# A fused mLSTM cell and squared-ReLU FFN on one NeuronCore: five groups of steps move to other places in the program

## The chip, the cores and the metric

The kernel runs on 1 core of one Trainium2 chip. The metric is the device time of one execution in microseconds (us). Before the change the median of 6 runs is 491.36 us, from 490.32 to 494.64.

A NeuronCore has five instruction streams. PE (TensorE) multiplies matrices into PSUM banks. DVE (VectorE), ACT (ScalarE) and POOL (GpSimd) do elementwise work. SP (SyncE) here only issues DMAs. Each stream runs in the order in which it was written, so an instruction that waits holds up all that stand behind it on its engine, and the engines wait for one another through semaphores.

## The reference

All inputs are float32. The attention part is a recurrence over 768 time steps for 4 batches x 8 heads, with head size 40:

```python
for t in range(S):
    m_new = np.maximum(f[t] + m, i[t])
    f_stab, i_stab = np.exp(f[t] + m - m_new), np.exp(i[t] - m_new)
    C = f_stab * C + i_stab * outer(v[t], k[t])      # 40 x 40 state of each head
    n = f_stab * n + i_stab * k[t]
    y[t] = sigmoid(o[t]) * (C @ q[t]) / np.maximum(np.abs(n @ q[t]), 1.0)
```

Its output is reordered to 3072 tokens x 320 features (8 heads x 40) and goes through an FFN: `h = max(x @ w_in, 0)`, `out = (h * h) @ w_out`, with w_in 320 x 2048 and w_out 2048 x 320. The launcher hands the weights over as 64-bit words: their raw bits are fetched as two 32-bit words each and put together on the chip.

## The kernel before, in words

**Tiling.** Time is cut into 24 chunks `s` = 0..23 of 128 tokens (6 per batch, batch by batch). Within a chunk the recurrence is written in its parallel form: scores k.q, weighted by decays, times the values, plus the state C carried from the chunk before times the queries. The FFN works on 12 groups `g` of two chunks.

**What is done for a chunk.** `load_part` and `load` fetch k, q, v; `transposes` turns k and q on PE, with the copies to SBUF on ACT; `load_A` brings the cumulated decays, broadcast to all partitions; `mask` (POOL) makes them causal; `weigh` takes their exponentials (ACT) and makes `vw`, the weighted values (POOL); `scores` is PE; `weighted` multiplies scores and weights (DVE); `attend` does the products with the values and with the state, on PE; `decay_old` is POOL; `half_tanh` is the output gate's sigmoid (ACT) on what `load_o` fetched; `normalise` makes the chunk's output x (DVE); `turn_rows` turns x on PE and copies it to `xT` on ACT. From chunk 4 on, other forms of the same steps are used (`attend_begin`, `attend_end`, `normalise_turned`), with turns by way of DRAM.

**Weights.** The class `Rounding` goes through 18 pieces: pieces 0 to 9 are w_in (0, 1, 3, 4, 5, 6, 8, 9 are 128 rows x 512 columns; 2 and 7 are `w_in2`, the last 64 rows, fetched by two DMAs), pieces 10 to 17 are w_out. Each piece has three steps that may stand far apart: `fetch` (SP: the DMA of the raw words), `words` (ACT: two instructions, lines 216 and 218) and `join` (DVE: three instructions, lines 227, 231, 232; then one POOL add, line 236, which writes the weight; and then the fetch of a later piece, since a raw buffer is free). Of the raw buffers three are in turn, and pieces 3, 7 and 11 use a fourth place inside `lent_t`.

**FFN.** `ffn1(g, pp)` is a quarter of x @ w_in for group g: 16 matmul passes at line 896 and 8 at line 907, into two PSUM banks of `ps_h` (3 banks). `relu_half` empties these banks on ACT and `square_half` squares. For groups 0 and 1 this is plain; from group 2 on FFN1 is `ffn1_open`, `ffn1_rows` and `ffn1_close`, and from group 1 on FFN2 is `ffn2_fast`. These need fewer products, at the price of sums of weights (`sums_of_weights(0..3)`, `sums_of_win`) and of activations (`sums`) on DVE. `sums_of_weights(3)` writes one quarter of w_out in place (line 961).

**Order.** Everything is in an order written out by hand, and each engine and SP's queue run in that order. There are three stretches:

1. The opening (lines 1148 to 1223): chunks 0 and 1 whole, chunk 2 begun, pieces 0 to 3 of the weights. `idle(n)` are n matmuls on zeros.
2. The loop over `u` = 0..7 (from line 1228): in each, a quarter of FFN1 of group 0 or 1, half of a chunk's attention (chunks 2 to 5), and pieces of the weights up to the count in `NEXT`. `rounding.step()` does words one piece ahead and a join.
3. The main loop over `n` (from line 1345): part n is (which, g, i), with `which` 1 for FFN1 and 2 for FFN2 of group g; the chunk is s = 6 + n // 4, and `at` = n % 4 says which of its steps go with the part.

The steps that the change touches: the fetch of piece 2 and `load_part(2, ...)` in SP's order; `load_A(3)` and `load_part(3, ...)`; `scores(0)`; `scores(2)`; `weigh(1)`; words and joins 1 to 3; `load_o(4)` to `load_o(7)` in the loop over u; `half_tanh(6)` and `half_tanh(7)`; the two POOL clears of the state buffers `C_flat` (line 1200); `sums_of_weights(3)` (line 961); and `spread_slots(2)` (three DMAs on POOL's queue).

Of the kernel before, what the change touches and what calls it, by code (L numbers as in the profile page):

```python
# [29 lines left out]
def kernel(  # L30
# [148 lines left out]
    class Rounding:  # L179
# [11 lines left out]
        def fetch(self):  # L191
            n = len(self.raws)
            if n == len(pieces):
                return
            dst, srcs = pieces[n]
            if n < LENT and n % NRAW == NRAW - 1:
                at = 2 * NPAIR * P
                raw = lent_t[:, at : at + 2 * WIDE].bitcast(I32).rearrange("p (c w) -> p c w", w=2)
            else:
                raw = conv.tile([P, WIDE, 2], I32, name="raw", bufs=NRAW - 1)  # L200
            self.raws.append(raw)
            for rows, src in srcs:
                to = raw[rows, : dst.shape[1]]
                if len(src.shape) == 4:
                    to = to.rearrange("p (a f) w -> p a f w", a=src.shape[1])
                nc.sync.dma_start(to, src)
# [200 lines left out]
    def load_o(s):  # L407
        b, c = divmod(s, NB)
        r, (s0, s1) = next((r, (a, z)) for r, (a, z) in enumerate(RUNS) if a <= s < z)
        if s == s0:  # L410
            st["og", r] = ld.tile([P, 4, H, D], F32, name="og")
        og = st.setdefault(s, {})["og"] = st["og", r][:, s - s0]
        nc.sync.dma_start(og, o_gate[b, :, c * P : (c + 1) * P, :].rearrange("h p d -> p h d"))
# [25 lines left out]
    def spread_mask(s):  # L439
        H2 = H // 2  # L440
        A = ps_h.tile([P, H2, P], F32, name="A_ps", tag="h_ps")
        nc.tensor.matmul(
            A[:], lhsT=ident_h[:], rhs=later_h[:].unsqueeze(1).to_broadcast([P, H2, P]), start=True, stop=True,
            skip_group_check=True,
        )
        st.setdefault(s, {}).setdefault("A", []).append(A)
# [688 lines left out]
    def idle(n):  # L1135
        t = ps_h.tile([P, W], F32, name="idle", tag="h_ps")
        for _ in range(n):
            nc.tensor.matmul(
                t[:], lhsT=zeros[:, :1].to_broadcast([P, P]), rhs=zeros[:, :1].to_broadcast([P, W]), start=True, stop=True,
            )  # L1140
# [5 lines left out]
    def load_part(s, i):  # L1146
        b, c = divmod(s, NB)
        dst, src = load_parts(s)[i]
        nc.sync.dma_start(dst, src[b, :, c * P : (c + 1) * P, :].rearrange("h p d -> p h d"))
# [10 lines left out]
    load_part(1, 2)  # L1160
    load_o(0)
    load_o(1)
    idle(12)
    transposes(0)
    idle(4)
# [3 lines left out]
    rounding.words()  # L1169
    store_A()  # L1170
    load_A(2)
    load_part(2, 0)
    load_part(2, 1)
    fetch(1)
    load_part(2, 2)
    fetch(1)
    spread_A(0)
    turn_gates(i_sb, b_T)
    rounding.join()
    load_A(3)  # L1180
    load_part(3, 0)
    load_part(3, 1)
    eA_turned = turn_gates(A_sb, eA_T, later=True)
    weigh(0)
    eA_turned()
    transposes(1, (False, True))
    spread_mask(1)
    spread_mask(1)
    spread_A(1)
    scores(0)  # L1190
    weigh(1)
    scores(1, (True, True))
    rounding.words()
    first.close()
    ffn = ctx.enter_context(tc.tile_pool(name="ffn", bufs=2))
    before = ExitStack()
# [2 lines left out]
    for x in C_flat:  # L1199
        nc.gpsimd.memset(x[:], 0.0)  # L1200
    C_old += [x[:, : 2 * PR * D1].rearrange("p (j i d) -> p j i d", i=2, d=D1) for x in C_flat]
    half_tanh(0)
    half_tanh(1)
    weighted(0)
    weighted(1)
    attend(0)
    rounding.join()
    load_part(3, 2)
    load_o(2)
    load_o(3)  # L1210
    rounding.words()
    normalise(0)
    attend(1)
    rounding.join()
    turn_rows(0)
    transposes(2)
    idle(2)
    turn_rows(1)
    rounding.words()
    scores(2)  # L1220
    weigh(2, masked=True)
    decay_old(2)
    rounding.join()


# [2 lines left out]
    for u in range(8):  # L1228
        s = 2 + u // 2
        relu_half()  # L1230
        if u % 2 == 0:
            if u == 0:
                ffn1(0, 0)
            else:
                if u == 2:
                    idle(3)
                if s - 1 < X_SQ:
                    turn_rows(s - 1)
                if u == 4:
                    square_half()  # L1240
                scores(s)
                ffn1(u // 4, u % 4)
            if u == 2:
                rounding.words()
                weigh(4, masked=True, vw=False)
                decays(4)
                rounding.words()
            weighted(s)
            if u == 0:
                mask(s + 1)  # L1250
                rounding.step()
            if u == 2:
                rounding.join()
                rounding.join()
                mask_W(4)
                values(4)
                rounding.words()
            else:
                if u == 0:
                    relu_half()  # L1260
                weigh(s + 1, masked=(u != 6), vw=(u == 6))
                if u == 4:
                    mask_W(5)
                square_half()
                if u > 0:
                    scale_q(s)
        else:
            if u == 1:
                half_tanh(2)
                half_tanh(3)  # L1270
            if u < 7:
                load_A(s + 2)
            for r in {1: (), 3: (5, 6), 5: (7,), 7: ()}[u]:
                load(r)
            if u == 5:
                for r in range(4, 8):
                    half_tanh(r)
            if s < X_SQ:
                attend(s)
            else:  # L1280
                attend_begin(s)
                attend_end(s)
                store_num(s)
            if u == 3:
                square_half()
            if u != 3:
                rounding.join(fetch=u < 7)
            if u == 1:
                load(4)
                values(s + 1)  # L1290
            if s < X_SQ:
                normalise(s)
            if u == 3:
                rounding.join()
            if u == 5:
                pair_up(7)
            if u == 7:
                load_A(7)
            if u > 4:
                load_num(s)  # L1300
            transposes(s + 1, (True, True))
            rounding.words()
            ffn1(u // 4, u % 4)
            if u != 3:
                square_half()
            if u == 5:
                decays(5)
            if u == 7:
                normalise_turned(4)
                store_rows(4)  # L1310
                rounding.fetch()
                rounding.join()
        if u < 4:
            load_o(4 + u)
        while rounding.done < NEXT[u]:
            if u == 1 and rounding.done + 1 == NEXT[u]:
                rounding.join()
            else:
                rounding.step()
        if u == 6:  # L1320
            load_squares(7)
        for x in WIN_SUMS.get(u, ()):
            sums_of_win(x)
# [21 lines left out]
    for n, (which, g, i) in enumerate(parts):  # L1345
# [3 lines left out]
            late = ctx.enter_context(tc.tile_pool(name="late", bufs=1, side="right"))  # L1349
        even = s % 2 == 0  # L1350
        fast = which == 1
        if at == 0 and even:
            do(scores, s)
            if n > 0:
                do(turn_kq, s + 1)
            do(weighted, s)
# [5 lines left out]
            rounding.join()  # L1362
        if at == 1:
            do(attend_begin, s)
            if even:
                do(lambda s: scores(s, ("h", "h")), s + 1)
            if fast:
                ffn1_rows(g, 0, True)
            do(attend_end, s)
            do(decays, s + 1)  # L1370
            do(mask, s + 1)
            if not even and not fast:
                do(turn_kq, s + 1)
            do(decay_C, s + 1)
            if not fast and not even:
                do(turn_squares, s - 1)
            if even and s > NB:
                do(load, s + 3)
            do(store_num, s)
            if n == 1:  # L1380
                normalise_turned(5)
                store_rows(5)
                turn_squares(4)
            if n == 5:
                load_rows(6)
            do(load_num, s)
            if n == 1:
                load_rows(5)
                weigh(7, masked=True)
                sums_of_win(2)  # L1390
            do(load_squares, s + 2)
            if even:
                do(load_A, s + 2)
# [4 lines left out]
        if n == 8:  # L1398
            sums(1, slice(0, NPAIR), (3,))
        if n == 9:  # L1400
            sums_of_weights(3)
            sums(1, slice(0, NPAIR), (4,))
            sums_of_weights(2)
            turn_squares(6)
# [67 lines left out]
            sums_of_weights(1)  # L1472
        if n == 3:
            turn_halves()
        if n in (9, 25):
            spread_slots(2 + n // 25)
        if at == 0:
            ffn1_square()
# [33 lines left out]
```

## Time and profile before

| what | before |
|---|---|
| time, median of 6 runs | 491.36 us |
| time, lowest to highest | 490.32 to 494.64 us |
| the profiled execution's own time | 489.87 us |
| its span, first to last instruction | 488.2 us |
| PE busy | 478.6 us (98%) |
| PE weight loads busy | 446.7 us (92%) |
| DVE busy | 339.2 us (69%) |
| ACT busy | 242.7 us (50%) |
| POOL busy | 225.8 us (46%) |
| mean granted TensorE clock | 0.996 |

The profile is one execution. Times in it count from its first instruction. A line of the timeline names start, length, engine, source line, operation, out<-in, shape and count, and in brackets the engine's idle time just before and what ended it. "PE" are matmuls, "PEld" the weight loads beside them, "SPq" the queue of SP. The difference of 1.7 us between the execution's own time and its span lies outside the instructions. The matmuls of float32 operands appear as two passes each.

### The profile page before, as it was taken

How to read it: one execution, taken by the hardware profiler on the slowest of the kernel's cores; microseconds unless marked ns; L12 is line 12 of the kernel's file. 1: busy time of each engine (PE TensorE's matmuls, PEld its weight loads, DVE VectorE, ACT ScalarE, POOL GpSimd, SP SyncE). 2: the span in 40 equal slices, each digit the busy share in tenths (PEclk: the TensorE clock that was granted, in tenths of full speed). 3: DMA queues.
4: the chain of work that ended last, by engine and by line, in shares of the span. 5: the costliest groups of instructions: out<-in, count | busy, mean ns of one | idle time of the engine just before them, and what ended most of it. 6: DMA issues, size and time to landing. Idle time of an engine off the chain costs nothing.

```text
span 488.2 us, 15402 instructions
## 1 busy us (share of the span) xinstructions
PE 478.6 (98%) x6227; PEld 446.7 (92%) x6229; DVE 339.2 (69%) x719; ACT 242.7 (50%) x534; POOL 225.8 (46%) x335
## 2 busy tenths in 40 slices
PE   9999999999999999999999999999999999999997
PEld 4877887779989999999999999998999999999997
DVE  7778768896986856857966956866956956635441
ACT  4479899534842741942742941742942650513300
POOL 5454534664689078089089077189074040020000
PEclk9989999999999999999999999999999999999999
DMA  8999998769999668769669759779646512200000
GB/s 180 195 233 239 306 212 206 207 120 210 190 141 219 123 113 219 139 112 213 130 110 220 132 93 214 144 129 206 121 93 164 122 48 83 56 21 10 1 28 27
DMA packets 192695, 69.92 MB, mean 143 GB/s; under 512 B 158128, under 2 KB 181360, under 8 KB 192624
## 3 DMA queue, kind: packets, MB, share of 16 engines
q1 hardware_dynamic: 186400, 58.68, 56.8%
q0 software_dynamic: 6080, 10.16, 9.4%
q8 instruction: 49, 0.80, 0.7%
q14 instruction: 22, 0.18, 0.1%
q10 hardware_dynamic: 144, 0.10, 0.1%
HBM read 55.69 MB, written 18.92 MB: 153 GB/s over the span
## 4 chain that ended last, share of the span: by engine, by line
PE 87%; DVE 4%; DMA 3%; ACT 2%; SPq 2%; issue 1%; POOL 0%; DVEq 0%; ACTq 0%; POOLq 0%
PE h_ps L980 34%; PE h_ps L1056 25%; PE h_ps L1089 7%; PE h_ps L896 5%; PE h_ps L934 4%; PE numT L746 3%; PE numT L727 2%; PE numT L757 1%; PE h_ps L907 1%; PE h_ps L579 1%; DMA raw<-in_moe_w_out_dram 1%; PE tp L579 1%; DMA a_rows<-A_sb 1%; DMA raw<-in_moe_w_in_dram 1%; PE tp L587 1%
## 5 line engine op out<-in xcount | busy, mean ns | idle before, releaser
L478 POOL TENSOR_SCALAR_AFFINE_SELECT A_bc<-A_bc 64x512 f32<-64x512 f32 x32 | 23.5, 733 | 89.0 <-ACT kq L496 71.0
L1070 ACT COPY r_sb<-h_ps 128x512 f32<-128x512 f32 x20 | 11.7, 586 | 85.5 <-PE h_ps L1056 85.5
L980 PE MATMUL h_ps<-T,S 128*128 128x160 f32 x352 | 51.7, 300 | 0.0
L980 PE MATMUL h_ps<-w_out,g 128*128 128x160 f32 x336 | 49.4, 303 | 0.7 <-DVE w_out L961 0.7
L980 PEld LDWEIGHTS h_ps<-T,S 128*128 128x128 f32 x352 | 48.9, 190 | 0.4 <-ACT g_c L1105 0.2
L980 PEld LDWEIGHTS h_ps<-w_out,g 128*128 128x128 f32 x336 | 46.1, 190 | 2.3 <-DVE w_out L961 0.9
L996 DVE TENSOR_TENSOR y_sb<-y_sb,h_ps 128x160 f32<-128x160 f32 x44 | 14.0, 319 | 45.3 <-PE h_ps L980 44.9
L1056 PE MATMUL h_ps<-xT,w_in 128*128 128x128 f32 x320 | 43.3, 278 | 0.0
L1056 PE MATMUL h_ps<-lent_t,w_in 128*128 128x128 f32 x320 | 42.3, 275 | 0.0
L1056 PEld LDWEIGHTS h_ps<-xT,w_in 128*128 128x128 f32 x320 | 39.2, 192 | 1.6 <-issue 1.2
L375 POOL DMA_DIRECT2D va<-in_v_dram x64 | 39.2, 619 | 1.4 <-DMA kq_rows<-in_k_dram 0.8
L1089 PE MATMUL h_ps<-xT,w_in 64*64 64x128 f32 x960 | 39.1, 272 | 0.0
L1056 PE MATMUL h_ps<-lent_t 128*128 128x128 f32 x320 | 39.0, 275 | 0.0
L1056 PEld LDWEIGHTS h_ps<-lent_t,w_in 128*128 128x128 f32 x320 | 38.9, 192 | 0.0
L1056 PEld LDWEIGHTS h_ps<-lent_t 128*128 128x128 f32 x320 | 37.3, 192 | 0.0
L509 ACT ACTIVATE A_bc<-A_bc,b_R 128x64 f32<-128x64 f32 (+1 forms) x128 | 35.7, 361 | 1.1 <-POOL A_bc L478 0.7
L1089 PEld LDWEIGHTS h_ps<-xT,w_in 64*64 64x64 f32 x960 | 34.8, 133 | 1.3
L780 DVE STREAM_TRANSPOSE tn<-numT 128x256 f32<-128x256 f32 x36 | 14.0, 428 | 30.2 <-PE numT L727 21.1
L896 PE MATMUL h_ps<-xT,w_in 128*128 128x256 f32 x128 | 31.2, 398 | 1.1 <-ACT g L920 0.8
L1048 POOL TENSOR_TENSOR lent_t<-xT 128x128 f32<-128x128 f32 (+1 forms) x18 | 14.7, 833 | 32.7 <-DVE xT L862 32.7
L896 PEld LDWEIGHTS h_ps<-xT,w_in 128*128 128x128 f32 x128 | 24.6, 199 | 5.5 <-POOL w_in L236 1.0
L980 PE MATMUL h_ps<-w_out,g_c 128*128 128x160 f32 x192 | 28.0, 302 | 0.0
(223 smaller groups left out, 1146.4 us busy)
## 6 DMA issues: line engine op xcount, KB each, us to landing
A_bc<-a_slots SPq DMA_DIRECT2D x32, 256.0 KB, 4.5
kq<-num_rows SPq DMA_DIRECT2D x80, 64.0 KB, 2.3
num_rows<-tn SPq DMA_DIRECT2D x18, 256.0 KB, 2.6
raw<-in_moe_w_out_dram SPq DMA_DIRECT2D x7, 640.0 KB, 5.6
kqT<-kq_rows SPq DMA_DIRECT2D x34, 128.0 KB, 4.0
og<-in_o_gate_dram SPq DMA_DIRECT2D x24, 160.0 KB, 4.7
x_rows<-x_sb SPq DMA_DIRECT2D x20, 192.0 KB, 3.0
xT<-x_rows SPq DMA_DIRECT2D x80, 48.0 KB, 3.7
```

The lines of the kernel that those rows point to most:

```text
L375: eng.dma_start(dst[HALVES[n], PR * (1 - late_keys) : PR * (2 - late_keys)], src[HALVES[late_keys], PR * m : PR * (m + 1)],)
L478: nc.gpsimd.affine_select(part, part, compare_op=ALU.is_ge, fill=-1e30, base=0, pattern=[[0, PR], [0, 2], [1, DP]], channel_multiplier=-1,)
L509: nc.scalar.activation(A[0][:, x, to], A[0][:, x, to], AF.Exp, bias=b_R[:, b, c, own, x : x + 1],)
L746: nc.tensor.matmul(d["numT"][m][HALVES[e], i, t0:], lhsT=va_w[s % NKQ][keys, at * D1 : at * D1 + DP], rhs=rhs, start=(s % NB == 0 and i == ...
L780: nc.vector.transpose(to[:, 2 * m : 2 * m + 2], d["numT"][m].rearrange("p c t -> p (c t)"))
L896: nc.tensor.matmul(hs[i][:, n, :], lhsT=w_in[:, a, fb * P : (fb + 1) * P], rhs=xT[:, :, a, :], start=(n == 0 and a == 0), stop=False,)
L934: nc.tensor.matmul(st["o_ps"][j], lhsT=st["g2", 0][:, fb, j * P : (j + 1) * P], rhs=w_out[:, fb, :], start=(fb == 0), stop=(fb == NF - 1),)
L980: nc.tensor.matmul(to, lhsT=lhsT[:, p], rhs=rhs[:, p, :], start=(start and p == 0), stop=(p == NPAIR - 1), skip_group_check=True,)
L996: add = lambda to, a, b: nc.vector.tensor_tensor(to, a, b, op=ALU.add)
L1048: sub = lambda to, a, b: eng.tensor_tensor(to, a, b, op=ALU.subtract)
L1056: nc.tensor.matmul(to[:, n, :], lhsT=lhsT[:, 4 * q + n, :], rhs=rhs, start=(start and n == 0), stop=True, skip_group_check=True,)
L1089: nc.tensor.matmul(to[cols, n, :], lhsT=w_in2[rows, 4 * q + n, cols], rhs=rhs, start=(start and n == 0), stop=True, skip_group_check=True,)
```

## The change

The program's instructions are the same in kind; they stand in other places.

- **Opening.** SP issues the fetch of piece 2 and chunk 2's k and q before `load_A(2)`, not after it. `load_A(3)` and chunk 3's k and q come behind `weighted(1)`. `scores(0)` stands before the masks of chunk 1. words 1 stand before `weigh(1)` and join 1 before `attend(0)`. The clears of `C_flat` stand before `weigh(1)`. words 2 stand right behind `weighted(1)` in ACT's order; words 3 stand behind `weigh(2)`. `transposes(2)` follows `turn_rows(1)`.
- **Loop over u.** `scores(2)` follows `ffn1(0, 0)`. `load_o(4)` to `load_o(7)` stand in u = 2 and u = 3, two in each, instead of one in each of u = 0..3. `half_tanh(6)` and `half_tanh(7)` leave u = 5.
- **Main loop.** `half_tanh(6)` and `half_tanh(7)` are in part 2. `sums_of_weights(3)` is in part 5, between `attend_begin` and `attend_end` of chunk 7, instead of part 9. `spread_slots(2)` is in part 12 instead of part 9.

```diff
     load_o(0)
     load_o(1)
+    fetch(1)
+    load_part(2, 0)
+    load_part(2, 1)
     idle(12)
...
     store_A()
     load_A(2)
-    load_part(2, 0)
-    load_part(2, 1)
-    fetch(1)
     load_part(2, 2)
     fetch(1)
     spread_A(0)
     turn_gates(i_sb, b_T)
     rounding.join()
-    load_A(3)
-    load_part(3, 0)
-    load_part(3, 1)
     eA_turned = turn_gates(A_sb, eA_T, later=True)
     weigh(0)
     eA_turned()
     transposes(1, (False, True))
+    scores(0)
     spread_mask(1)
     spread_mask(1)
     spread_A(1)
-    scores(0)
-    weigh(1)
-    scores(1, (True, True))
-    rounding.words()
     first.close()
...
         nc.gpsimd.memset(x[:], 0.0)
...
+    rounding.words()
+    weigh(1)
+    scores(1, (True, True))
     half_tanh(0)
     half_tanh(1)
     weighted(0)
+    rounding.join()
+    attend(0)
     weighted(1)
-    attend(0)
+    load_A(3)
+    load_part(3, 0)
+    load_part(3, 1)
+    rounding.words()
+    normalise(0)
+    attend(1)
     rounding.join()
     load_part(3, 2)
     load_o(2)
     load_o(3)
-    rounding.words()
-    normalise(0)
-    attend(1)
-    rounding.join()
     turn_rows(0)
-    transposes(2)
     idle(2)
     turn_rows(1)
-    rounding.words()
-    scores(2)
+    transposes(2)
     weigh(2, masked=True)
     decay_old(2)
+    rounding.words()
     rounding.join()
...
             if u == 0:
                 ffn1(0, 0)
+                scores(2)
...
             if u == 5:
-                for r in range(4, 8):
-                    half_tanh(r)
+                half_tanh(4)
+                half_tanh(5)
...
-        if u < 4:
-            load_o(4 + u)
+        if u in (2, 3):
+            load_o(2 * u)
+            load_o(2 * u + 1)
...
+        if n == 2:
+            half_tanh(6)
+            half_tanh(7)
...
             do(attend_begin, s)
+            if n == 5:
+                sums_of_weights(3)
...
         if n == 9:
-            sums_of_weights(3)
             sums(1, slice(0, NPAIR), (4,))
...
-        if n in (9, 25):
+        if n in (12, 25):
             spread_slots(2 + n // 25)
```

## The prediction, made before the result was known

> **What bounds the kernel now.** I read the page first, then PE's waits, then the chain that ended last for the first 110 us, then the timelines of ACT, SP, DVE and PE around the places where the chain leaves PE, and last the windows with the granted clock.
>
> ```profile
> PE 478.6 (98%) x6227; PEld 446.7 (92%) x6229; DVE 339.2 (69%) x719; ACT 242.7 (50%) x534; POOL 225.8 (46%) x335
> ```
>
> PE is the bound: busy for 98% of a span of 488.2 us. Moving steps can only win PE's idle time, a slowed clock and the fillers. PE's waits, the longest first:
>
> ```profile
> PE tp L870 <- ACT xT L875: 1.4, 1, 1.4
> PE idle L1138 <- DVE zeros L1133: 1.0, 1, 1.0
> PE h_ps L896 <- ACT g L920: 0.8, 1, 0.8
> ```
>
> The second is the start of the run. Smaller ones are 0.7 for line 961 on DVE and 0.2 for a copy to xT at 61.98.
>
> The chain says what is behind the first: from 14.13 it runs through SP's queue, the raw words of piece 2, ACT, and only at 26.06 into PE.
>
> ```profile
> 14.13 0.34 SPq L434
> ...
> 16.27 2.84 SPq L206
> 19.15 4.22 DMA raw<-in_moe_w_in_dram
> ...
> 26.06 1.24 PE tp L587 x16
> ```
>
> ACT stands 6.00 us in front of words 2, and behind it wait the two copies to xT that PE needs. Later it stands 1.18 us in front of words 7, behind which the emptying of PSUM banks (line 920) waits, and 2.14 us for piece 10.
>
> ```profile
> 23.46 0.66 ACT L216 ACTIVATE lent_t<-raw 128x512 f32<-128x512 f32 x1 [6.00 <-DMA raw<-in_moe_w_in_dram]
> ...
> 44.10 0.68 ACT L216 ACTIVATE mag<-lent_t 128x512 f32<-128x512 f32 x1 [1.18 <-DMA lent_t<-in_moe_w_in_dram]
> 44.69 0.65 ACT L218 ACTIVATE low<-lent_t 128x512 f32<-128x512 uint32 x1
> 45.25 1.06 ACT L920 ACTIVATE g<-h_ps 128x512 f32<-128x512 f32 x2
> ```
>
> The windows give the clock. In 24.0 to 27.0 PE was busy 1.75 of 3.00 us (58%), and it then ran 3.4 us at half clock; in 44.1 to 47.5 it was busy 2.56 of 3.40 (75%), and the clock stayed.
>
> ```profile
> 24.00:27.00 3.00, 1.75 (x22) 1.34 (x22) 1.93 (x5) 2.42 (x6) 0.81 (x1) 1.00 0.96 362
> 27.00:30.40 3.40, 3.40 (x12) 2.57 (x11) 1.61 (x4) 3.37 (x10) 0.46 (x1) 0.50 0.94 188
> ...
> 44.10:47.50 3.40, 2.56 (x23) 2.24 (x24) 2.62 (x4) 3.40 (x7) 1.64 (x2) 1.00 1.17 284
> ```
>
> **The opening, part by part.** *Piece 2's fetch earlier.* SP's last issue before its wait for a_rows ends at 12.99, and it stands until 14.13. The two fetches of piece 2 (issues 2.84 and 0.61, landing 4.22 after the later one) now go there instead of 16.27. With issues of 0.6 to 1.4 they land near 18.5 to 19.5 instead of 23.38. Words 2 (1.2 us on ACT) end near 20.5. Chunk 2's k and q follow (1.09 and 0.58); `load_A(2)` moves behind four issues, from 14.13 to about 16 to 18.5, and with the 5.3 us to landing that its neighbours show, from 19.4 to 21.5 to 24. Behind it wait mask 2 on POOL (1.35 us, at 20.89 so far), then join 2's add (1.27), chunk 2's exponentials (ACT, at 28.16 so far). They are needed near 26 and 28.5, so the cover is 2 us; were the load still later, each us would fall on the first FFN1 part.
>
> *Words 1 before weigh 1; join 1, attend 0 sooner; scores 0 first.* Scores 0 (half of 2.06 us) put chunk 1's mask products 1.0 us later, so weigh 1 (2.3 us) starts at 14.3 instead of 13.31; in front of it words 1 (1.3 us) fit into just that time. On DVE, weighted 0 starts at 12.6 instead of 14.41, and join 1 (1.6 us) fits into the 2.15 us that DVE stood idle. Chunk 1's x, done at 23.8, comes near 23.0. The clears (0.72 on POOL) go into a gap of 1.55 and cost nothing. The xT copies then wait for no words: turn of chunk 1 near 23.3 instead of 25.09, `transposes(2)` (1.09) behind it, first FFN1 part at 25.1 instead of 27.23. That is 2.1 us; without a 1.4 us gap before it I expect no half clock, which spares half of 3.4, 1.7 us.
>
> Join 2's fetch (piece 6) now stands ahead of chunk 3's v and two gate loads in SP's queue and can hold them until join 2 ends, near 25.2; SP, still held by chunk 3's k and q until 26.0 in the profile (3.43 at 22.57), should come no sooner: 0, and for each us that join 2 is later, sigmoids 2 and 3 are later too.
>
> *Scores 2 behind the first FFN1 part*: 1.2 us of PE work inside the count either way. Weighted 2 (1.29 on DVE) now comes between scores 2 and the products with it, covered by the state products ahead of them on PE (1.05 + 0.89 = 1.94). Without that cover it costs up to 1.3.
>
> *Where this gain goes.* From 27.23 PE worked 17.9 us until it was ready for the third FFN1 part at 45.13; now 17.9 - 1.7 + 1.2 = 17.4, so from 25.1 it is ready at 42.5. But that part started at 45.97 for another reason: words 7 could start at 44.10, then came bank emptying and PE. Raw words 7 stand behind the same DMAs as before, in another order (piece 5 before the decays, k and q of chunk 3; piece 6 before chunk 3's v and two gate loads). They land earlier only by transfer time no longer wasted. The windows of 1 us from 14 to 21 have DMA shares of 0.82, 0.85, 0.91, 0.90, 1.24, 0.25 and 0.82: 1.45 us free. Lower bound: 0, if the free time only moves. Upper: 42.5 instead of 45.97, 3.5 us, where PE's own work binds. I take 1.7: nearest to the 1.45 measured, and a little for raw words 7 no longer standing right behind raw words 6.
>
> **Loop over u.** Moving `load_o(4)` and `load_o(5)` (0.43 and 0.59 of SP, 160 KB each) out of u = 0 and 1 brings raw words 10 forward, so ACT's 2.14 us wait shrinks by more than the 1.7 and the 0.22 us wait of PE at 61.98 goes: 0.2. In u = 2 and 3 these loads stand ahead of chunk 5's decays (line 434 at 54.81), which ACT takes at 62.73: some 0.8 us of SP and transfer, against the 1.7 won. Sigmoids 6 and 7 take 1.9 us off ACT at 70.12; no PE wait stood there: 0.
>
> **Main loop.** Part 5: line 961 took 1.96 us (its neighbours at 954 and 956 took 1.48), put where DVE stood 2.00 us idle, then another 0.90:
>
> ```profile
> 116.62 0.78 DVE L780 STREAM_TRANSPOSE tn<-numT 128x256 f32<-128x256 f32 x2 [2.00 <-PE numT L727]
> ...
> 136.70 1.96 DVE L961 TENSOR_TENSOR w_out<-w_out 128x1280 f32<-128x1280 f32 x1
> ```
>
> ```profile
> 138.71 2.44 PE L980 MATMUL h_ps<-w_out,g 128*128 128x160 f32 x16 [0.68 <-DVE w_out L961]
> ```
>
> Cost 0; without the cover, 2.0. In part 9 PE's 0.68 us goes; next in DVE's order are the sum at 138.58 and T2 at 139.99, needed by PE at 145.3 and 143.2 and now 1.9 earlier: 0.7 won. Sigmoids 6 and 7 in part 2 (1.9 us) lie in ACT's 7.58 us before 108.26: 0. `spread_slots(2)` (0.59 + 1.20 on POOL) leaves 143.39 for about 151, ahead of chunk 12's decays by tens of us; mask 10 moves from 157.07 by up to 1.8, and its exponentials are first needed past 170: 0.
>
> **Sum.** 1.7 + 0.2 + 0.7 = 2.6 us off the profiled execution's 489.87 us: 487.3. That execution is 1.5 us below the median of the runs, 491.36, so the median should come to 488.8 us, 0.53% less. About 0.5%, 2.5 us, is what a measurement of this kernel can tell from no change, so the forecast lies at that bound.
>
> **A rule against the row.** The Trainium skill, page "TensorE: Matmul & The Clock Gate", Part 1, says that the array falls to half clock after at least one idle window of about 3.4 us. By that rule the wait in front of the third FFN1 part (44.3 - 42.5 = 1.8 us) costs no clock, and the sum stays at 2.6. The row shows half clock after a window that was 58% busy; by the row such a wait can cost 1.7, and the sum would be 0.9. The row decides; hence the rivals below.
>
> **Rivals.**
> - *PE's own work binds as far as part 3* (raw words 7 in time): 3.5 + 0.2 + 0.7 = 4.4, 487.0 us. For it: 1.45 us of free transfer time, and ACT 2.68 us less in front of words 5. Against: the set of transfers ahead is the same.
> - *Hidden anyway*: raw words 7 land at 44.0 as before, the opening's gain is all waited away; 0.2 + 0.7 remain: 490.5 us. For it: DMA share near or above 1 from 21 to 28 and 40 to 47.
> - *Slower: half clock in front of the third FFN1 part.* If raw words 7 do not land before about 43.5, PE, ready at 42.5, stands 3 us or more; a window under 58% busy follows, and PE runs at half clock for one window (1.7) or, if the gap spreads over two, two (3.4). With 0.9 won, that is +0.8 to +2.5: 492.2 to 493.9 us. Against: the fillers and the turn of chunk 2 lie in the same window.
>
> **How the numbers follow.** Forecast, gain of 1.8 to 3.4 (488.0 to 489.6): 0.46, of it 0.30 below 488.9 and 0.16 above. PE-bound: 0.17, faster. Hidden: 0.23, no change. Slower: 0.14, of it 0.13 past 0.5% with the half that spreads and the misses of cover above (2.0 at part 5, 1.3 at weighted 2), 0.01 within. Sum: faster 0.47, within 0.40, slower 0.13. Range: from 486.7 (PE-bound, less 0.3 for the scatter of medians) to 492.4, with the lower end of the slower case; about 1 in 10 beyond each end.
>
> **What would show it.** Right: ACT's 6.00 us before words 2 down to some 2 and no clock of 0.50 near 27 to 30; first FFN1 matmul near 25; third near 44.3, released by ACT line 920; no PE wait on line 961, and DVE's idle before 116 filled. Wrong: a granted clock of 0.5 between 40 and 50; raw words 7 landing at 44 still; PE waiting on xT or mask 2; DVE late for the turns of chunk 7.

## The result, and the profile after

| what | before | after |
|---|---|---|
| time, median (runs) | 490.35 us (78) | 487.85 us (38) |
| time, lowest to highest | 487.44 to 494.64 us | 484.87 to 491.82 us |
| ratio, 95% interval | | 0.9952, 0.9939 to 0.9966 |
| the profiled execution's own time | 489.87 us | 486.68 us |
| its span | 488.2 us | 485.0 us |
| PE busy | 478.6 us | 475.8 us |

The change takes off 2.5 us (0.48%, between 0.34% and 0.61%); between the two profiled executions it is 3.2. The forecast was 488.8, with a range of 486.7 to 492.4. Five executions of the calls below, four of 612 to 1243 us and one of 495.75, stand outside the ratios and the clock counts.

PE's line of the page, and the head of PE's waits (line waited for, total us, times, longest):

```profile
PE 475.8 (98%) x6227; PEld 445.1 (92%) x6229; DVE 341.1 (70%) x719; ACT 243.3 (50%) x534; POOL 229.3 (47%) x335
```

```profile
PE h_ps L1056 <- issue: 1.1, 1, 1.1
PE idle L1138 <- DVE zeros L1133: 1.0, 1, 1.0
PE numT L746 <- issue: 0.7, 1, 0.7
```

The same places on PE: the first and the third FFN1 part before, the first after, and then FFN2 of group 0 before and after (from the chains).

```profile
27.23 5.29 PE L896 MATMUL h_ps<-xT,w_in 128*128 128x256 f32 x16
45.97 3.69 PE L896 MATMUL h_ps<-xT,w_in 128*128 128x256 f32 x16 [0.84 <-ACT g L920]
```

```profile
24.45 3.62 PE L896 MATMUL h_ps<-xT,w_in 128*128 128x256 f32 x16
```

```profile
89.26 4.54 PE h_ps L934 x16
```

```profile
86.06 4.54 PE h_ps L934 x16
```

PE does the same 6227 matmuls in 2.8 us less. The 3.4 us at half clock before would be 1.7 of that; the rest is not assigned, since the ends of matmuls are modelled. The 1.4 us in front of the turn (line 870), the 0.8 in front of the third FFN1 part and the 0.7 on line 961 are gone. New are, at the top, 1.1 us at line 1056, where PE waits for nothing that the profile names, and 0.4 us in the third part, shown below. The 0.7 at line 746 had a like of 0.8 before.

ACT's timeline, at words 2, the emptying of banks ahead of the third FFN1 part, and words 10:

```profile
20.16 0.66 ACT L216 ACTIVATE lent_t<-raw 128x512 f32<-128x512 f32 x1 [1.99 <-DMA raw<-in_moe_w_in_dram]
...
40.61 1.06 ACT L920 ACTIVATE g<-h_ps 128x512 f32<-128x512 f32 x2
...
49.42 0.80 ACT L216 ACTIVATE mag<-raw 128x640 f32<-128x640 f32 x1 [1.26 <-POOL w_in L236]
```

Words 2 waited 1.99 us, not 6.00. Words 7 ran at 39.48 with no wait in front of them (44.10 before, after 1.18), so line 920 emptied its banks at 40.61, 4.64 us sooner. Words 10 waited 1.26 us for POOL's add of an earlier piece, not 2.14 for their transfer. In the place of words 7's lateness PE has this, at the third part:

```profile
42.63 0.70 PE L896 MATMUL h_ps<-xT,w_in 128*128 128x256 f32 x2
43.73 3.29 PE L896 MATMUL h_ps<-xT,w_in 128*128 128x256 f32 x14 [0.40 <-POOL w_in L236]
```

It starts 3.34 us sooner (45.97 before), stops after two passes, and ends its main passes 2.64 sooner (49.66 to 47.02). What stands behind the stop, the chain that ended last shows; from 24.2 to 43.7 it now stays off PE, and from 28.3 on nearly all of it is DVE:

```profile
41.52 0.70 DVE mag L232
...
42.35 1.33 POOL w_in L236
...
43.73 3.29 PE h_ps L896 x14
```

That is join 6 and its POOL add. The chain comes to it on DVE, by a join at 28.3, weighted 2 at 30.38, two more joins and the normalising of chunk 2 (37.5 to 40.2). What stands last at the third part is now DVE's order, not raw words. Part of this is length, as DVE's and then POOL's timelines show:

```profile
24.65 0.43 DVE L231 TENSOR_SCALAR lent_t<-lent_t 128x512 int32<-128x512 int32 x1
32.10 1.20 DVE L231 TENSOR_SCALAR mag<-mag 128x512 int32<-128x512 int32 x1
41.05 0.43 DVE L231 TENSOR_SCALAR mag<-mag 128x512 int32<-128x512 int32 x1
```

```profile
31.73 1.29 POOL L472 TENSOR_SCALAR_AFFINE_SELECT A_bc<-A_bc 128x1024 f32<-128x1024 f32 x1
```

Line 231 took 0.43 us at 24.65 and 41.05, where POOL was idle, and 0.84, 1.20, 0.99 and 1.38 at 28.78, 32.10, 35.76 and 42.58, where POOL computed beside it; lines 833 and 834 likewise took 0.18 each from 21.17, and 0.82 and 0.66 at 38.05 and 38.90. Between 20 and 50 us of before, lines 231, 833 and 834 were long only once, 1.37 us at 32.42, also beside POOL. By these lengths some 2.9 us of the chain up to 42.2 are such stretching, an estimate; that POOL is the cause was not tested.

The windows (PE, PEld, DVE, ACT, POOL busy, then the clock, DMA share and GB/s) that answer to those of before:

```profile
21.00:24.40 3.40, 3.09 (x26) 2.11 (x27) 3.22 (x9) 1.54 (x4) 1.09 (x1) 1.00 1.03 272
24.40:27.80 3.40, 3.40 (x18) 2.91 (x16) 1.33 (x3) 3.40 (x12) 1.36 (x2) 1.00 0.98 358
```

PE is 91% busy ahead of the first FFN1 part, which starts at 24.45 (27.23 before), and the clock stays. Last, part 5 on DVE, and PE in part 9 and at the new stop:

```profile
111.45 1.65 DVE L961 TENSOR_TENSOR w_out<-w_out 128x1280 f32<-128x1280 f32 x1
113.42 0.78 DVE L780 STREAM_TRANSPOSE tn<-numT 128x256 f32<-128x256 f32 x2 [0.32 <-PE numT L727]
```

```profile
132.40 4.61 PE L980 MATMUL h_ps<-w_out,g 128*128 128x160 f32 x32
...
151.73 1.05 PE L1056 MATMUL h_ps<-xT,w_in 128*128 128x128 f32 x8 [1.14 <-issue]
```

Line 961 fills DVE's idle 2.00 us, of which 0.32 are left, and nothing is late behind it. In part 9 PE goes through without a stop. But the place where FFN2 of group 0 starts was 3.20 us sooner (89.26 to 86.06), and the end is 3.2 sooner too: of the wait won in part 9 nothing reaches the end, and 1.14 us are lost at 151.73.

### The profile page after: what moved, and what is told of

Read it like the earlier page. It is cut to its first block, busy times and chain, and to the rows that moved or that the text cites. A ratio compares the mean times of both kernels' runs of the same rounds, so it can differ in the third digit from the quotient of the medians.

```text
span 485.0 us, 15404 instructions
## 1 busy us (share of the span) xinstructions
PE 475.8 (98%) x6227; PEld 445.1 (92%) x6229; DVE 341.1 (70%) x719; ACT 243.3 (50%) x534; POOL 229.3 (47%) x335
## 4 chain that ended last, share of the span: by engine, by line
PE 89%; DVE 6%; issue 1%; DMA 1%; ACT 1%; SPq 1%; POOL 0%; DVEq 0%; POOLq 0%
PE h_ps L980 34%; PE h_ps L1056 24%; PE h_ps L1089 7%; PE h_ps L896 4%; PE h_ps L934 4%; PE numT L746 3%; PE numT L727 2%; PE numT L757 1%; PE h_ps L907 1%; PE h_ps L579 1%; PE tp L587 1%; PE tp L579 1%; PE tp L553 1%; PE hp L660 1%; DMA kq<-num_rows 1%
## 5 line engine op out<-in xcount | busy, mean ns | idle before, releaser
L478 POOL TENSOR_SCALAR_AFFINE_SELECT A_bc<-A_bc 64x512 f32<-64x512 f32 x32 | 25.9, 809 | 87.8 <-ACT kq L496 70.2
L1056 PEld LDWEIGHTS h_ps<-xT,w_in 128*128 128x128 f32 x320 | 39.2, 192 | 2.6 <-issue 2.2
L896 PE MATMUL h_ps<-xT,w_in 128*128 128x256 f32 x128 | 29.8, 383 | 0.5 <-POOL w_in L236 0.4
L896 PEld LDWEIGHTS h_ps<-xT,w_in 128*128 128x128 f32 x128 | 23.5, 190 | 4.5 <-POOL w_in L236 1.3
```

The source lines that it names most:

```text
L478: nc.gpsimd.affine_select(part, part, compare_op=ALU.is_ge, fill=-1e30, base=0, pattern=[[0, PR], [0, 2], [1, DP]], channel_multiplier=-1,)
L896: nc.tensor.matmul(hs[i][:, n, :], lhsT=w_in[:, a, fb * P : (fb + 1) * P], rhs=xT[:, :, a, :], start=(n == 0 and a == 0), stop=False,)
L1056: nc.tensor.matmul(to[:, n, :], lhsT=lhsT[:, 4 * q + n, :], rhs=rhs, start=(start and n == 0), stop=True, skip_group_check=True,)
```

## The experiments

All times are medians; "ratio" is to the kernel before, with its 95% interval. Intervals are some 0.2% (1 us) wide to each side, so parts under 1 us are read from traces. All kernels do the whole computation. Each execution also lists its mean granted clock: a window of 3.4 us at half clock takes some 0.0035 off it, which tells the number of such windows where no trace was kept.

**The changed kernel again, and its halves.** r1 is the changed kernel. r2 is before with the changed opening and the place of `scores(2)`; r3 is the reverse, the changed kernel with the opening of before. r4 is before with line 961 alone moved:

```diff
+            if n == 5:
+                sums_of_weights(3)
...
         if n == 9:
-            sums_of_weights(3)
```

> The changed kernel as it is. Its trace shows PE 3.0 us ahead at 62 us of the old trace, 3.2 us at the second FFN stage, and one stop of PE of 1.14 us at line 1056 (151.7 us) that no semaphore explains. Theory: the whole change is worth about 3.9 us of removed waits, and the stop of 1.14 us takes a part back; it belongs to the program and comes again in this profile. Rival: the stop is chance and is gone in this profile; then the span is 1 us shorter. Ratio to the kernel before about 0.995.

> The opening and the place of scores 2 alone are as in the change; gate loads, sigmoids, sum of w_out, spread of slots as before. Theory: the opening makes nearly all of it: third FFN1 part complete about 2.6 us earlier, 2.4 to 2.9 us off the time, ratio 0.994 to 0.995. Rival from the prediction's middle term: 1.7 us (0.9965). Rival: without the moved gate loads raw words 7 land late again (about 42.5 to 44) and PE waits for the emptying of banks: at most 1 us off.

> All of the change but the opening and the place of scores 2. Theory: 0.7 us for the sum of w_out and 0.2 for the wait at 61.98 us: 0.9 us off, ratio about 0.998; the half clock near 27 to 30 us and the wait of 0.84 us near 46 us are there as before. Rival: the moved gate loads carry the gain in the transfers; then the wait near 46 us goes here too and 1.5 to 2 us are won.

> The kernel before with the one in-place sum of w_out moved from part 9 to part 5. Theory: PE's wait of 0.68 us on line 961 goes and nothing takes its place: 0.7 us off, ratio 0.9986. Rival: DVE is late for the turns of chunk 7 or the next sums, and PE waits there: no change or up to 1.3 us slower.

| | median | ratio | third part | fifth part | FFN2 of group 0 | half clock in the profile |
|---|---|---|---|---|---|---|
| before | | | 45.97 | 61.98 | 89.26 | 27.0, 3.4 us |
| after | 487.85 | 0.9952 (0.9939 to 0.9966) | 42.63 | 58.96 | 86.06 | none |
| r1_after | 487.39 | 0.9946 (0.9922 to 0.9969) | 42.62 | 58.94 | 86.05 | none |
| r2_open_only | 488.06 | 0.9968 (0.9943 to 0.9992) | 42.68 | 59.76 | 86.86 | none |
| r3_rest_only | 488.73 | 0.9981 (0.9951 to 1.0011) | 44.81 | 60.98 | 88.08 | none |
| r4_sum_only | 489.07 | 0.9975 (0.9952 to 0.9998) | 46.03 | 61.69 | 88.80 | 27.4, 3.4 us |

The opening alone gives the whole gain at the third part. The gate loads are the difference between r2 and the changed kernel at the fifth part, 0.80 us: in r2 ACT waited 2.84 us for piece 10's raw words.

```profile
52.61 0.81 ACT L216 ACTIVATE mag<-raw 128x640 f32<-128x640 f32 x1 [2.84 <-DMA raw<-in_moe_w_out_dram]
```

By time the halves add to about the whole, but none is told from its neighbour. In r4 PE no longer waits for line 961, and stands 1.64 us at line 1056. And r3, with the old opening and no half clock, starts its third part 1.2 us sooner than before: the clock is a matter of the single execution. There PE waited for chunk 2's x ahead of it:

```profile
42.85 0.41 PE L870 MATMUL tp<-ident,x_sb 128*128 128x128 f32 x2 [0.90 <-DVE x_sb L840]
...
44.81 0.67 PE L896 MATMUL h_ps<-xT,w_in 128*128 128x256 f32 x2
```

By the mean clock of each execution, r2 kept full clock in 11 of 12, r3 in 7 of 12 and before in 15 of 35 of this call. Where it was kept, the medians are 488.0 (r2), 487.3 (r3), 488.2 (before) and 487.2 us (r1, 11 executions). So in r2 the time shows the opening through the clock, and hardly where the clock stays, unlike the traces; with so few executions that is a hint only.

**Raw words of piece 2 late.** The changed kernel, with these issues put back:

```diff
-    fetch(1)
-    load_part(2, 0)
-    load_part(2, 1)
     idle(12)
...
     load_A(2)
+    load_part(2, 0)
+    load_part(2, 1)
+    fetch(1)
```

> The changed kernel, with the fetch of piece 2 and chunk 2's k and q behind the decays of chunk 2 again, as before; all else as changed. Theory: ACT waits some 5 to 6 us in front of words 2 again, the first FFN1 part starts near 27 us instead of 24.45, and the third near 44 to 45 instead of 42.63; 1 to 2.5 us slower than the changed kernel, ratio to the kernel before 0.997 to 1.000. Rival: what counts is that piece 5 is ahead of chunk 3's loads; then the first part is late but the third starts near 42.6 to 43 again, at most 0.5 us slower than the changed kernel.

> The same kernel as r5_raw2_late, run once more since its profiled execution was of no use (span 1241 us). Theory of the prediction: words 2 wait some 6 us on ACT again, the turn of chunk 1 stands behind them, the first FFN1 part starts at 26.5 to 27.5 us and the third at 44 to 46 us. Rival: the first part moves, but the third starts within 1 us of 42.6 all the same, because raw words 7 land by 41 and PE has slack for it.

r5: 487.92 us, ratio 0.9984 (0.996 to 1.0009). Its profiled execution, with a span of 1241 us, is not used. r10: 488.02 us, span 486.3, and PE's timeline has:

```profile
25.66 0.66 PE L553 MATMUL tp<-ident,kq 128*128 128x128 f32 x4 [1.21 <-ACT xT L875]
...
44.28 0.70 PE L896 MATMUL h_ps<-xT,w_in 128*128 128x256 f32 x2
```

Words 2 waited 6.91 us on ACT, and PE 1.21 for the copy to xT behind them. The first part, at 26.15, is 1.70 us later than in the changed kernel, the third 1.65, FFN2 of group 0 1.66 (87.72 to 86.06). Raw words 7 landed at 39.46, as in the changed kernel (39.38). So what the opening loses or wins goes on through the third part in full: raw words 7 do not stop it. The rival fell. How much of it shows in the time stays open: the medians differ by 0.1 to 0.6 us (487.92 and 488.02 to 487.39 and 487.85), the ratios by 1.6 to 1.9, with intervals that overlap. In r10's trace PE has no stop at line 1056, and the end is 1.3 us later.

**Chunk 3's loads early again.** The changed kernel with `load_A(3)` and chunk 3's k and q ahead of piece 5:

```diff
     rounding.join()
+    load_A(3)
+    load_part(3, 0)
+    load_part(3, 1)
     eA_turned = turn_gates(A_sb, eA_T, later=True)
```

> The changed kernel, with chunk 3's decays, k and q ahead of piece 5 in the queue of SP again. Theory: words 5 wait for their raw words (near 34 us instead of 29), raw words 7 land near 41.5 to 42 instead of 39.4, the third FFN1 part starts 0.5 to 1.5 us later; the first part keeps its 24.45; 0.5 to 1.5 us slower than the changed kernel. Rival: the same transfers stand ahead of raw words 7 either way, they land near 39.4, and the time is that of the changed kernel.

486.62 us, ratio 0.995 (0.993 to 0.997): the same as the changed kernel. The profiled execution had what the prediction's slower rival describes, in an earlier place:

```profile
31.84 1.09 PE L649 MATMUL dC<-vw,kq 128*128 128x82 f32 x8 [0.92 <-DVE g_c L601]
```

```profile
30.20:33.60 3.40, 2.48 (x23) 2.36 (x22) 3.30 (x6) 0.43 (x1) 2.48 (x2) 1.00 0.98 291
33.60:37.00 3.40, 3.40 (x18) 3.40 (x18) 3.25 (x8) 2.86 (x7) 1.29 (x2) 0.50 0.95 177
```

Weighted 2 (line 601) came 0.92 us late, and half clock, for two windows (33.6 to 40.4), followed one that was 73% busy; the third part began at 45.80. It is a thing of some executions: 9 of 12 kept a mean clock of 0.999 or more.

**The clock held.** Before, with more matmuls on zeros in front of chunk 1's turn:

```diff
-    idle(2)
+    idle(8)
     turn_rows(1)
```

> The kernel before with idle(8) instead of idle(2) in front of the turn of chunk 1, so that the array has work in the gap of 1.42 us. Theory: the half clock near 27 to 30 us does not come, the first FFN1 part takes 3.6 instead of 5.3 us, the second starts 1.3 to 1.7 us earlier, but the third still starts when raw words 7 have landed (44 to 46 us): at most 0.5 us off the whole time. Rival: PE's own work is what counts and the spared 1.7 us stay to the end: ratio 0.9965.

489.0 us, ratio 0.9981 (0.9961 to 1.0001). In the profile there is no half clock; the third part starts at 43.47, 2.50 us sooner than in before, FFN2 of group 0 at 86.98, 2.28 sooner.

```profile
43.47 0.67 PE L896 MATMUL h_ps<-xT,w_in 128*128 128x256 f32 x2
```

Nothing else than fillers was changed, but raw words 7 also landed at 40.46 (44.00 in the profile of before). So of the 3.34 us that the whole change gains at the start of the third part, 1.2 (r3) to 2.5 (r7) come in profiles with the old opening whose clock does not fall; what of that is the clock and what is earlier data, these profiles do not separate. In the time only 0.5 to 0.9 us show, for the six fillers cost where the clock would have stayed: executions at full clock have a median of 488.92, those of before 488.2.

**Gate loads back**, one in each of u = 0..3, the rest as changed:

```diff
-        if u in (2, 3):
-            load_o(2 * u)
-            load_o(2 * u + 1)
+        if u < 4:
+            load_o(4 + u)
```

> The changed kernel with the gate loads of chunks 4 to 7 one in each of u = 0 to 3 again. Theory: as with the opening alone, ACT waits near 2.8 us for the raw words of piece 10, and PE's fifth FFN1 part starts near 59.7 instead of 58.95: 0.8 us slower than the changed kernel. Rival: the sigmoids 6 and 7, taken off ACT, made that difference; then the fifth part starts at 58.95 as in the changed kernel.

486.37 us, ratio 0.9934 (0.9912 to 0.9956). ACT waited 3.40 us for piece 10, and the fifth part started at 59.55 instead of 58.96.

```profile
52.39 0.82 ACT L216 ACTIVATE mag<-raw 128x640 f32<-128x640 f32 x1 [3.40 <-DMA raw<-in_moe_w_out_dram]
```

The 0.6 us are plain in the trace and lost in the time, whose interval overlaps the changed kernel's; it is not shown to be better or worse.

**Line 961 back in part 9**, the rest as changed (r4's diff the other way round):

> The changed kernel with w_out's sum (line 961) back in part 9; nothing else differs, and PE's own order is the same. Theory of the prediction: PE waits for line 961 again in part 9, some 0.7 us, and the end comes 0.7 us later: about 0.9965 of the kernel before, where the changed kernel stood at 0.9946 to 0.9952. Rival: what the earlier sum wins in part 9 is taken back some 20 us later, where PE stands 0.3 to 1.6 us at line 1056 for its own instructions in every variant with the earlier sum but not in the profile of before; then the wait of 0.7 us comes back, the stop at line 1056 is under 0.3 us, and the time stays within 0.2 us of the changed kernel's.

488.21 us, ratio 0.9979 (0.9948 to 1.0011), which does not tell the two theories apart. PE's timeline:

```profile
135.34 2.44 PE L980 MATMUL h_ps<-w_out,g 128*128 128x160 f32 x16 [0.51 <-DVE w_out L961]
...
151.82 1.05 PE L1056 MATMUL h_ps<-xT,w_in 128*128 128x128 f32 x8 [0.46 <-issue]
```

The wait is back, 0.51, and the stop at line 1056 is down from 1.14 to 0.46: the sum, 0.97, is within 0.2 of what it was. Over all usable profiles of this case, PE's own instruction fetches (the instruction queue of 49 packets of 16 KB, which is 12456 matmuls and weight loads by 256) go with the stop. The count is that of PE instructions in the trace when the fetch was issued that came last ahead of it:

| line 961 in | profile | count | stop at line 1056, us |
|---|---|---|---|
| part 9 | before; r12; r2; r7; r9 | 3097; 3097; 3082; 3021; 3090 | 0; 0; 0; 0; 0.46 |
| part 5 | r10; r1; r6; r8 | 3067; 3098; 3132; 3148 | 0; 0.32; 0.58; 0.79 |
| part 5 | after; r3; r4; r11 | 3168; 3177; 3234; 3249 | 1.14; 1.02; 1.64; 1.11 |

The stops counted are those for which the profile names nothing; in r2 and r7 PE also stood 0.51 us at line 1056, near 146.3, for POOL (line 1051). With the fetch by instruction 3098 the stop is at most 0.46 us, from 3132 on it is 0.58 to 1.64. The mean is 0.09 us where line 961 is in part 9, and 0.83 where it is in part 5: 0.7 more, as much as the wait that was won (0.2 to 0.7). That the fetch causes the stop, and that the wait in part 9 gives it its time, fits all 13 profiles but is an inference; no run here moved the fetch by itself. What does not need it: from the start of FFN2 of group 0 to the last instruction it is 398.3 to 399.6 us in the five profiles with line 961 in part 9, and 398.3 to 399.7 in the eight with it in part 5, some 399.0 in the mean of each. The move shows no gain there.

**Without fillers.** The changed kernel without `idle(2)` in the opening and `idle(3)` in front of the third part:

```diff
-    idle(2)
     turn_rows(1)
...
-                if u == 2:
-                    idle(3)
```

> The changed kernel without the two fillers (idle of 2 in the opening, idle of 3 in front of the third FFN1 part), 5 matmuls on zeros that compute nothing. Each execution lists its mean granted clock, and one window of 3.4 us at half clock lowers it by 0.0035 to 0.004: 0.996 or 0.997 is one window, 0.993 two. By the row of before (a window that was 58% busy was followed by half clock) PE then stands 1.2 us of a window of 3.4 ahead of the third part and 0.7 ahead of the second turn, so a third to half of the executions should show 0.997 or less, and the median comes to 488.5 or more (+1 us or more on the changed kernel). Rival, by the rule that only a window that is idle throughout slows the clock: no execution under 0.999, and the time within 0.4 us of the changed kernel, since its PE waits for x and not for the fillers there.

487.24 us, ratio 0.9945 (0.9925 to 0.9964): as the changed kernel. PE waited 0.69 and 0.97 us for the two turns, its poorest window of 3.4 us was 71% busy, and all 9 executions kept a clock of 0.999 or more. The rival held: such gaps alone did not lower the clock in these nine.

**Before again**, for a second profile:

> The kernel before, unchanged, for a second profile of it. Theory: half the gain of the change is clock. In the timed executions of before the mean clock falls into three groups, 1.0 (median 488.0 to 488.4 us), 0.996 to 0.997 (489.0 to 489.8) and 0.993 (491.1), while nearly all of the changed kernel's are at 0.999 to 1.0 (487.4 to 487.7); so this profile should show half clock at 27 to 34 us in zero, one or two windows of 3.4 us, and its third FFN1 part should start 1.2 to 2.0 us later for each. Rival: the third part starts at 45 to 46 whatever the clock does, because of raw words 7. The stop at line 1056: if it belongs to the change, PE has none there in this profile; if it is chance of each execution, 0.3 to 1.6 us.

489.27 us. Two windows of it, and ACT ahead of its third part:

```profile
24.40:27.80 3.40, 1.95 (x23) 1.42 (x23) 1.95 (x5) 3.40 (x8) 1.27 (x1) 1.00 1.06 372
27.80:31.20 3.40, 3.40 (x10) 2.77 (x9) 2.35 (x5) 3.40 (x12) 0.63 (x1) 0.50 1.17 226
```

```profile
43.36 1.09 ACT L920 ACTIVATE g<-h_ps 128x512 f32<-128x512 f32 x2 [0.39 <-PE h_ps L907]
```

Half clock comes again, one window, after one that was 57% busy. But raw words 7 landed at 41.41, not 44.00; ACT waited for PE, not PE for ACT, and PE ran into the third part at 45.70 without a gap. In this execution PE's own work, slowed by the clock, sets the third part. No stop at line 1056.

**The clock over all executions.** Mean clock, and the median time, of the 85 executions of before that were timed beside these runs, and of 49 of the changed kernel:

| mean clock | before | changed |
|---|---|---|
| 0.999 or 1.0 (no window) | 28: 488.2 us | 46: 487.6 us |
| 0.995 to 0.997 (one) | 32: 489.5 us | 3: 490.8 us |
| 0.992 or 0.993 (two) | 25: 491.1 us | none |
| all | 85: 489.5 us | 49: 487.7 us |

Two thirds of the executions of before lose clock, one in sixteen of the changed kernel; in the call with r1 20 of 35 and none of 11. Of 1.9 us between these medians 0.6 remain where the clock stays (0.9 in the call with r1, 488.18 to 487.24). The other 1.3 to 1.4 us go with the loss of clock: the half clock itself, and the late data that bring it on, which these numbers do not separate.

## Why the prediction was right, and which steps were wrong

*The opening's 2.1 us and the clock: right.* The wait for words 2 came to 1.99 us, the clock stayed, and the first part began at 24.45 instead of 27.23, 2.78 sooner where 2.1 was worked out: chunk 1's x was done at 22.66 and not 23.0, and its turn started at 22.81 and not 23.3. r10 shows the mechanism of the wait, with piece 2 late; its clock stayed all the same. The price of half clock, 1.7 a window and 3.4 for two, is a little above the 1.3 and 2.9 in the table above, which hold late data too.

*The third part held back by raw words 7, so only 1.7 us (0 to 3.5): wrong.* That step failed. PE was ready at 42.5 by the prediction, and at 42.63 it started. The working took 44.00, the landing of raw words 7 in the profile of before, for a property of the order of transfers. In the twelve other usable profiles of this case they landed between 38.35 and 42.48; in the four of them with the old opening (r3, r4, r7, r12) between 40.46 and 42.48. The limit belonged to that execution. The term measured 3.34 at the start and 2.64 behind the new 0.40 stop, which lies on DVE's order (joins, weighted 2) and was not foreseen. So the rival "PE's own work binds" told the mechanism, and its 3.5 was some 0.9 too much.

*Why the time came out near the sum all the same.* The median of before is not the profiled execution: its executions are spread over no, one and two windows of half clock. The opening's 2.6 in the pair of profiles is more than the sum's 1.7; against that, the last term of 0.7 did not reach the end. That these differences nearly cancel, and 2.5 came out beside 2.6, is in part luck.

*Wait at 61.98, gate loads, 0.2: small.* The fifth part came 3.02 us sooner, 0.38 more than the main passes of the third; r2 and r8 put the gate loads at 0.8 and 0.6 in the trace. Both are below what the times tell.

*Part 5 at no cost: right.* 1.65 us went into 2.00 of idle time. *Part 9, 0.7 won: won there, not kept.* The wait went, and a stop of 0 to 1.6 us at line 1056 came, 0.83 in the mean against 0.09. The trace of before had no such stop, and the prediction had no term for it.

*Covers: they held, one by less than was counted.* The load of A(2) landed at 23.18 (21.5 to 24 was given), mask 2 on POOL waited 4.13 for it, and no PE instruction was later for it; weighted 2 was covered but for 0.14 us of PE, 31.08 to 31.22. The prediction counted 1.94 us of state products as cover; in the traces the second of them, line 649, itself waits for weighted 2 (the 0.92 of r6 stands there), so only the first counts.

*The slower rival: rare.* Neither of the two profiles of the changed kernel lost clock; 3 of its 49 executions did, where in the program no trace shows. It did occur once in a variant (r6), two windows, 3.2 us at the third part.

*The rule and the row.* The Trainium skill, page "TensorE: Matmul & The Clock Gate", Part 1, has half clock behind at least one idle window of some 3.4 us. In these profiles no such window was idle throughout, and half clock came behind windows 34%, 53%, 57% and 73% busy (r4, before, r12, r6); so if idle means idle throughout, the rule is contradicted. But the row's reading, that some 58% busy is enough, fell as well: in r3 and r10 a window of 3.4 us was 49% busy, and the clock stayed. The page also says that the window runs freely, so that it depends on where in it the work falls when the clock changes; with that, equal programs that lose no, one or two windows agree. What share of a window is enough was not settled.

## What to carry to other kernels

Before a landing time or a clock in one profile is made the limit of a sum, look at a second profile of the same kernel: here the one number that capped the forecast was off by 2.6 us in the next execution. Read the mean granted clock of every timed execution as well as the time; the part of a gain that comes from clock shows as a share of executions, not as a shift of all. And when a wait of half a microsecond is removed from the bounding engine, look further on (here some 16 us) for what used the wait.

## What had not been expected of the hardware

PE stood up to 1.64 us at line 1056 with nothing in the profile that it waited for, next to a fetch of its own instructions. The Trainium skill, page "Runtime: NRT & Kernel Launch", section "Instruction fetch mechanics", says that instructions come in blocks of 16 KiB, 256 at a time, and that the cost of crossing is mostly hidden. The blocks agree (49 packets, 0.80 MB); beside the later fetches PE stood 0.6 to 1.6 us here, and that the fetch is the reason is inferred.

The same fetch of raw words 7 landed between 38.35 and 44.00 us over these profiles, and half clock came in some executions of a kernel and not in others, so two profiles of one program differ by more than the change made by most parts of it.
